# A spectral mixing layer and a gated feed-forward on one core: the order of loads, stores and weight sums in the opening

## The chip, the core and the metric

The kernel runs on one core of a Trainium2 chip. The metric is device time in microseconds, the median of several runs. A core has TensorE (PE in the profile, its weight loads PEld), VectorE (DVE), ScalarE (ACT), GpSimd (POOL) and SyncE (SP). Each engine takes its instructions in the order in which the kernel gives them; an instruction that waits holds all behind it on that engine. Transfers are issued by SyncE, ScalarE (their queues are SPq and ACTq) or GpSimd (POOLq), and the issue stands in the engine's order too.

## The reference

```python
def _attn_ref(x):                       # x: 8 x 3008 x 256
    X = np.fft.fft(x, axis=1)
    X = np.fft.fft(X, axis=2)
    return X.real.astype(np.float32)

def _moe_ref(x, w_in, w_out):           # 24064 x 256, 256 x 2048, 2048 x 256
    h = x @ w_in
    g = h * np.cos(h)
    return (g @ w_out).astype(np.float32)
```

The real part of a two-dimensional Fourier transform of each of 8 batches, over the 3008 positions and the 256 channels, goes through an input matrix, a gate h·cos(h) and an output matrix. All is float32.

## The kernel before, in words

**The transform over channels is folded into the weights.** `fold_weights(e, n)` (line 564) multiplies 512 columns of `w_in` by a cosine (`e` = 0) or sine (`e` = 1) matrix and leaves the result in `WC` or `WS`: four TensorE records of 512 columns and a ScalarE copy (lines 577, 583). For `e` = 1, row 0 belongs to the middle channel and is kept apart: VectorE copies it to `nrow[n]` (581), `send_wn(n)` (587) writes it to DRAM and `take_wn(n)` (591) reads it back across partitions into `wn`, four columns for each n. `load_w(n)` fetches the columns of `w_in`.

**The transform over positions is 47 times 64.** For batch 0, `load_x(b, p)` (189) loads half p of x, 16 of 32 columns from each of two sides, over SyncE (one column over GpSimd). `chunk(c)` (867) calls `fold(b, c, e)` (287): sums and differences of four columns on VectorE, and a ScalarE copy of one column (292). `first_half(b, c)` (414) multiplies the chunk by a 47-point matrix on TensorE and copies it to `zs` (450, 451); the chunk `DIRECT` (number 7) does without the fold. `middle(b, p)` (325) treats channel 128 of a whole half of x. `store_z(b, c, far)` (457) writes a chunk to DRAM: the near part (four of 24 output groups) first, over GpSimd for chunks 0 to 3 and over ScalarE and SyncE for the rest, the far part later over SyncE. `load_z` (482) reads it back with the axes exchanged, and `second_half(b, g)` (490) does the 64-point part for one of six groups of output rows: eight TensorE records (497), a ScalarE copy (508 or 514) and, for group 0 of batch 0, a small VectorE copy (512).

**The feed-forward runs in steps.** A step is one group of up to 256 rows by 256 of the 2048 inner columns: 8 batches x 6 groups x 8 = 384 steps. A step's accumulator H is seeded with 0.25 plus the product of middle channel and row weights: by ScalarE in `seed(s)` (629, 635) from `nb` and `wn`, or for the first two steps by VectorE and one-row matmuls in `fill_first` and `seed_first` (643, 647; 651). `mm1` (660, 665) adds the two matrix products; ScalarE and VectorE compute h·cos(h) (676 to 731); `mm2` (733, 755) multiplies by `w_out`. That matrix is used in sums of its quarters, which `combine_w2(f0, f1)` (617, 625) makes on VectorE for the inner columns f0 to f1 (eight in all) after `load_w2`. `combine_w2` is four instructions for each call.

**The order is written out by hand.** Lines 879 to 920 give the opening: `keep_busy` (603, matmuls on constants), the weight sums, the chunks, the stores, `combine_w2(0, 2)`, `load_z`, the later loads, `combine_w2(2, 4)` and `(4, 6)`, then `second_half(0, 0)`. The prologue (936 to 973) interleaves the first three steps by hand; `spread_norm` (524) broadcasts a row for them. The loop (988) runs three steps deep: step t starts `mm1` of step t while `mm2` of step t − 3 runs. Lists hold what else a step issues: `opening`, `todo`, `between`, `early` (weight sums in steps 3 and 4) and `aside`, GpSimd work that is made to start behind a given VectorE instruction of the step (`beside`, 979). `transform(b)` (535) puts batch b's loads, folds and halves into these lists; batch 1's first loads (`load_later_x`, 165) go out from step 2 on, over GpSimd for p = 0.

Of the kernel before, what the change touches and what calls it, by code (L numbers as in the profile page):

```python
# [29 lines left out]
XP = 4 * IP  # L30
# [104 lines left out]
def kernel(  # L135
# [29 lines left out]
    def load_later_x(b, p, s, set_):  # L165
# [4 lines left out]
        for k in range(7):  # L170
# [8 lines left out]
            queue = nc.gpsimd if b == 1 and p == 0 else nc.sync  # L179
# [9 lines left out]
    def load_x(b, p):  # L189
        xv = xs[p][0 : 16 * STEP].rearrange("(e g) c -> e g c", g=STEP)  # L190
        i0 = XP * p
        def load(queue, g, c0, c1, cols, **more):
            for m in range(3):
# [3 lines left out]
                    in_=x_r[b, 16 * m : 16 * m + k, cols],  # L197
# [12 lines left out]
    wr = [  # L210
# [3 lines left out]
    wr = [[w[:, 512 * i : 512 * i + 512] for i in range(2)] for w in wr]  # L214
# [5 lines left out]
    def load_w(q):  # L220
        for i in range(2):
            nc.sync.dma_start(
                out=wr[q][i],
                in_=moe_w_in[128 * i : 128 * i + 128, 512 * q : 512 * q + 512],
            )
# [22 lines left out]
    load_w(0)  # L248
# [8 lines left out]
    load_x(0, 0)  # L257
# [3 lines left out]
    load_x(0, 1)  # L261
# [3 lines left out]
    load_w(2)  # L265
# [21 lines left out]
    def fold(b, c, e):  # L287
# [3 lines left out]
        if e == 0:  # L291
            nc.scalar.copy(out=fv[:, 0, :, 0], in_=xv[:, :, 0])
# [164 lines left out]
    def store_z(b, c, far):  # L457
# [15 lines left out]
        for e in range(2):  # L473
            queue = nc.sync if far or (e == 0 and c in (4, 7)) else nc.scalar
# [60 lines left out]
    def transform(b):  # L535
# [28 lines left out]
    def fold_weights(e, n, tag="M"):  # L564
        W = WS if e else WC
        pw = psum("pw", tag)
        for i in range(2):
# [6 lines left out]
            )  # L574
        cols = slice(512 * n, 512 * n + 512)
        if e:
# [3 lines left out]
            nrow[n] = spool.tile([128, 512], FP, tag="pq", bufs=8, name="nrow")  # L580
            nc.vector.tensor_copy(out=nrow[n][0:1, :], in_=pw[0:1, :])
        else:
            nc.scalar.copy(out=W[:, cols], in_=pw)

    wds = {}

    def send_wn(n):
        wds[n] = dpool.tile([1, 512], FP, tag="wd", bufs=4, name="wd")
        nc.sync.dma_start(out=wds[n], in_=nrow[n][0:1, :])

    def take_wn(n):
        nc.sync.dma_start(
# [23 lines left out]

    def combine_w2(f0, f1):
        add, sub = ALU.add, ALU.subtract
        for dst, a, b, op in (
            (vx[:, 0], wv[:, 0, 1], wv[:, 0, 0], sub),  # L620
            (vx[:, 1], wv[:, 0, 1], wv[:, 1, 1], add),
            (vx[:, 2], vx[:, 0], wv[:, 1, 1], add),
# [454 lines left out]
```

## Time and profile before

| | |
|---|---|
| median of three runs | 1958.84 us (1954.87 to 1960.34) |
| the profiled execution, its own time | 1954.01 us |
| span of its profile | 1952.2 us |
| mean granted clock of TensorE | 0.994 |
| DMA, mean over the span | 46 GB/s |
| DMA between 5 and 10 us | 279 GB/s |

A profile line is read as: start and duration in us, the engine, the line of the kernel, the instruction, what it writes and reads, shape, how often; in brackets the idle time of the engine before it and what ended that. TensorE works one float32 matmul off in two records. Groups of one line (by shape) show their total and the mean in ns. The granted clock is a share of full speed.

### The profile page before, as it was taken

How to read it: one execution, taken by the hardware profiler on the slowest of the kernel's cores; microseconds unless marked ns; L12 is line 12 of the kernel's file. 1: busy time of each engine (PE TensorE's matmuls, PEld its weight loads, DVE VectorE, ACT ScalarE, POOL GpSimd, SP SyncE). 2: the span in 40 equal slices, each digit the busy share in tenths (PEclk: the TensorE clock that was granted, in tenths of full speed). 3: DMA queues.
4: the chain of work that ended last, by engine and by line, in shares of the span. 5: the costliest groups of instructions: out<-in, count | busy, mean ns of one | idle time of the engine just before them, and what ended most of it. 6: DMA issues, size and time to landing. Idle time of an engine off the chain costs nothing.

```text
span 1952.2 us, 30563 instructions
## 1 busy us (share of the span) xinstructions
PE 1927.7 (99%) x9534; PEld 1693.5 (87%) x9534; DVE 1780.4 (91%) x3348; ACT 1530.1 (78%) x2884; POOL 397.4 (20%) x465
## 2 busy tenths in 40 slices
PE   7999999999999999999999999999999999999998
PEld 3888889888998889988899888988889888898887
DVE  4889999999999998999989999899999999999998
ACT  3688878888788788887878888788887888788775
POOL 5022202222022211222112221122211222111101
PEclk8999999999999999999999999999999999999999
DMA  8221131012200121101211122110231000110000
GB/s 219 77 57 37 49 91 26 19 39 65 67 24 23 41 76 52 25 24 46 82 37 27 26 53 75 34 31 24 52 84 30 24 22 24 54 28 10 12 22 22
DMA packets 160753, 89.36 MB, mean 46 GB/s; under 512 B 109172, under 2 KB 155403, under 8 KB 158123
## 3 DMA queue, kind: packets, MB, share of 16 engines
q1 hardware_dynamic: 158655, 85.37, 16.8%
q0 software_dynamic: 1536, 1.81, 0.4%
q8 instruction: 76, 1.25, 0.3%
q14 instruction: 86, 0.70, 0.1%
q10 hardware_dynamic: 400, 0.23, 0.0%
HBM read 50.07 MB, written 37.28 MB: 45 GB/s over the span
## 4 chain that ended last, share of the span: by engine, by line
PE 96%; DVE 1%; DMA 1%; SPq 0%; issue 0%; ACT 0%; ACTq 0%; DVEq 0%
PE M L755 57%; PE H L665 34%; PE pb L497 2%; PE pz L387 2%; DMA w<-in_moe_w_out_dram 0%; PE pz L347 0%; DMA xp<-in_x_dram 0%; PE pz L445 0%; PE pw L568 0%; DVE r L710 0%; DVE S L721 0%; SPq L862 0%; PE H L651 0%; PE M L387 0%; SPq L195 0%
## 5 line engine op out<-in xcount | busy, mean ns | idle before, releaser
L755 PE MATMUL M<-S,VX 128*128 128x256 f32 (+1 forms) x2304 | 612.3, 375 | 0.0
L755 PEld LDWEIGHTS M<-S,VX 128*128 128x128 f32 x2304 | 437.8, 190 | 49.9
L696 ACT ACTIVATE r<-H 128x512 f32<-128x512 f32 (+1 forms) x384 | 226.1, 589 | 265.0 <-DVE h L681 265.0
L706 ACT ACTIVATE r<-r 128x1024 f32<-128x1024 f32 (+1 forms) x384 | 394.7, 1028 | 22.9 <-DVE r L700 18.9
L665 PE MATMUL H<-pq,WC 128*128 128x256 f32 (+1 forms) x1536 | 396.1, 381 | 1.8 <-ACT H L635 1.8
L665 PE MATMUL H<-pq,WS 128*128 128x256 f32 (+1 forms) x1536 | 389.4, 376 | 0.0
L755 PE MATMUL M<-r,w 128*128 128x256 f32 (+1 forms) x1536 | 387.7, 375 | 0.0
L635 ACT ACTIVATE H<-nb,wn 128x256 f32<-128x256 f32 (+1 forms) x764 | 362.0, 474 | 16.1 <-DVE r L710 1.3
L681 DVE TENSOR_TENSOR h<-ew,H 128x512 f32<-128x512 f32 (+1 forms) x384 | 258.9, 674 | 103.6 <-PE H L665 73.2
L665 PEld LDWEIGHTS H<-pq,WC 128*128 128x128 f32 x1536 | 284.7, 191 | 52.9 <-ACT r L696 15.8
L755 PEld LDWEIGHTS M<-r,w 128*128 128x128 f32 x1536 | 300.2, 196 | 28.3 <-issue 0.7
L665 PEld LDWEIGHTS H<-pq,WS 128*128 128x128 f32 x1536 | 292.6, 191 | 34.5 <-ACT ew L676 0.5
L700 DVE SCALAR_TENSOR_TENSOR r<-r,H 128x512 f32<-128x512 f32 (+1 forms) x384 | 258.6, 673 | 30.0 <-ACT r L696 13.6
L676 ACT ACTIVATE ew<-H 128x512 f32<-128x512 f32 (+1 forms) x384 | 225.8, 588 | 61.8 <-PE H L665 53.2
L807 POOL TENSOR_TENSOR cb<-cb,mr 128x256 f32<-128x256 f32 (+3 forms) x188 | 158.3, 852 | 518.1 <-DVE S L731 479.9
L721 DVE TENSOR_TENSOR S<-r 128x512 f32<-128x512 f32 (+1 forms) x384 | 259.0, 674 | 0.1
L710 DVE SCALAR_TENSOR_TENSOR r<-H,r 128x512 f32<-128x512 f32 (+1 forms) x384 | 255.9, 667 | 3.0 <-ACT r L706 2.5
L700 DVE SCALAR_TENSOR_TENSOR r<-r,h 128x512 f32<-128x512 f32 (+1 forms) x384 | 258.5, 673 | 0.0
L710 DVE SCALAR_TENSOR_TENSOR r<-h,r 128x512 f32<-128x512 f32 (+1 forms) x384 | 258.0, 672 | 0.0
L696 ACT ACTIVATE r<-h 128x512 f32<-128x512 f32 (+1 forms) x384 | 236.0, 615 | 0.0
L306 POOL TENSOR_TENSOR xs<-xp 113x512 f32<-113x512 f32 x112 | 143.2, 1278 | 446.4 <-DVE S L731 443.2
L755 PE MATMUL M<-S,w 128*128 128x256 f32 (+1 forms) x768 | 225.6, 375 | 1.1 <-DVE S L731 1.1
(103 smaller groups left out, 1581.5 us busy)
## 6 DMA issues: line engine op xcount, KB each, us to landing
out_dram<-ob SPq DMA_DIRECT2D x728, 32.0 KB
xp<-in_x_dram SPq DMA_DIRECT2D x250, 56.0 KB
z<-zd SPq DMA_DIRECT2D x8, 1280.0 KB
zd<-zs SPq DMA_DIRECT2D x224, 40.0 KB
nb<-nd SPq DMA_DIRECT2D x40, 128.0 KB
zd<-zs SPq DMA_DIRECT2D x224, 8.0 KB
xp<-in_x_dram SPq DMA_DIRECT2D x52, 48.0 KB
w<-in_moe_w_out_dram SPq DMA_DIRECT2D x4, 512.0 KB
```

Source lines behind the costliest of these rows:

```text
L306: return nc.gpsimd.tensor_tensor(out=xs2[e][0:XL], in0=xv[:, 0], in1=xv[:, 1], op=ALU.subtract if e else ALU.add,)
L635: nc.scalar.activation(out=s.H[:, u * T : u * T + T], in_=s.nb[:, 0:T], func=AF.Copy, bias=0.25, scale=wn[:, f : f + 1],)
L665: nc.tensor.matmul(s.H[:, u * T : u * T + T], lhsT=W[:, 128 * f : 128 * f + 128], rhs=s.pq[:, e * T : e * T + T], start=False, stop=True, ...
L676: nc.scalar.mul(out=s.ew[:, 0 : 2 * s.T], in_=s.H[:, 0 : 2 * s.T], mul=2.0)
L681: nc.vector.tensor_tensor(out=s.h[:, 0 : 2 * T].rearrange("p (u t) -> p u t", u=2)[:, :, ::-1], in0=s.ew[:, 0 : 2 * T].rearrange("p (u t) ...
L696: nc.scalar.activation(out=r, in_=h, func=AF.Copy, bias=BIG, scale=1.0)
L700: nc.vector.scalar_tensor_tensor(out=r, in0=r, scalar=-BIG, in1=h, op0=ALU.add, op1=ALU.subtract)
L706: nc.scalar.activation(out=r, in_=r, func=AF.Sin, bias=0.0, scale=SIN_SCALE)
L710: nc.vector.scalar_tensor_tensor(out=r, in0=h, scalar=-0.25, in1=r, op0=ALU.add, op1=ALU.mult)
L721: return nc.vector.tensor_tensor(out=sv[:, 0:2], in0=gv[:, 2:3].to_broadcast([128, 2, T]), in1=gv[:, 0:4:3], op=ALU.subtract,)
L755: nc.tensor.matmul(acc[key][m // 2][:, 256 * (m % 2) : 256 * (m % 2) + T], lhsT=w, rhs=a, start=first, stop=s.fp == 7, skip_group_check=True,)
L807: return nc.gpsimd.tensor_tensor(out=o, in0=a, in1=b, op=ALU.subtract if less else ALU.add)
```

## The change

- `load_x` takes a range of columns and a side. The second side goes over ScalarE's queue (for a range that starts at 0); the first half of x goes ahead of the first weight columns; the second half is loaded in two ranges. Contiguous runs are up to 4096 bytes instead of 1024 in one piece.
- `load_w(0..2)` is one transfer instead of two. `load_w(2)` moves from the first loads to a place behind `load_z` and `load_w2(2, 4)`.
- Eight filling matmuls instead of two; the two weight sums of n = 0 leave the start: the sine one stands before the fifth chunk, its row copy and the cosine one behind the last. The sine sum of n = 2 moves into the prologue, the cosine one to its end; the cosine sum of n = 3 from step 4 to step 5.
- Chunks run in the order 0 to 5, 7, 6 instead of 0 to 3, 7, 4 to 6. The copy of one column moves from ScalarE to VectorE.
- Near stores: ScalarE issues two instead of six, SyncE six.
- The row weights go to DRAM and back over GpSimd's queue, each pair together.
- `second_half(0, 0)` comes ahead of `combine_w2(2, 4)`. The sums for columns 4 to 8 run on GpSimd, one column in each of steps 3 to 6.
- Of batch 1's first loads seven stay on GpSimd; the others go to SyncE, at step 3 at the earliest. `load_w2(6, 8)` moves behind the far part of z.

```diff
-            queue = nc.gpsimd if b == 1 and p == 0 else nc.sync
+            queue = nc.gpsimd if b == 1 and p == s == set_ == 0 else nc.sync
...
-    def load_x(b, p):
+    def load_x(p, c0, c1, side):
...
+        queue = nc.scalar if side and not c0 else nc.sync
...
-        load(nc.sync, 0, 0, XP, slice(i0, i0 + XP), max_dma_last_dim=1024)
-        c0 = 0 if p else 1
-        load(nc.sync, 3, c0, XP, slice(64 - i0 - c0, 64 - i0 - XP, -1))
-        if p == 0:
+        if side == 0:
+            load(nc.sync, 0, c0, c1, slice(i0 + c0, i0 + c1), max_dma_last_dim=4096)
+            return
+        skip = 1 if p == c0 == 0 else 0
+        load(queue, 3, c0 + skip, c1, slice(64 - i0 - c0 - skip, 64 - i0 - c1, -1))
+        if skip:
             load(nc.gpsimd, 3, 0, 1, slice(32, 33))
...
     nc.sync.dma_start(out=LCS, in_=LCS_dr.ap())
-    load_w(0)
...
-    load_x(0, 0)
+    for side in range(2):
+        load_x(0, 0, XP, side)
...
-    load_x(0, 1)
+    load_w(0)
+    for c0 in (0, XP // 2):
+        for side in range(2):
+            load_x(1, c0, c0 + XP // 2, side)
     load_bj(0, 512)
     load_w(1)
     load_w2(0, 2)
-    load_w(2)
...
-            nc.scalar.copy(out=fv[:, 0, :, 0], in_=xv[:, :, 0])
+            nc.vector.tensor_copy(out=fv[:, 0, :, 0], in_=xv[:, :, 0])
...
-            queue = nc.sync if far or (e == 0 and c in (4, 7)) else nc.scalar
+            queue = nc.scalar if not far and e and c in (5, 6) else nc.sync
...
-                at(o + k, load_later_x, b, p, k % 2, k // 2)
+                at(max(o + k, LAG) if b == 1 and k else o + k, load_later_x, b, p, k % 2, k // 2)
...
-        nc.sync.dma_start(out=wds[n], in_=nrow[n][0:1, :])
+        nc.gpsimd.dma_start(out=wds[n], in_=nrow[n][0:1, :])
...
-        nc.sync.dma_start(
+        nc.gpsimd.dma_start(
             out=wn[:, 4 * n : 4 * n + 4], in_=wds[n].rearrange("o (q p) -> (o p) q", p=128)
...
-    keep_busy(2, "H", 512)
-    fold_weights(1, 0, "H")
-    fold_weights(0, 0, "H")
-    order = [c for c in range(NCH) if c < 4] + [DIRECT] + [c for c in range(4, NCH) if c != DIRECT]
+    keep_busy(8, "H", 512)
+    order = [0, 1, 2, 3, 4, 5, DIRECT, 6]
     folded = [c for c in order if c != DIRECT]
     chunk(folded.pop(0))
     for k, c in enumerate(order):
-        if c == DIRECT:
+        if k == 4:
             middle(0, 1)
-        elif folded:
+        if c != DIRECT and folded:
             chunk(folded.pop(0))
+        if k == 4:
+            late = fold_weights(1, 0, "H")
+            keep_fold(*late)
         first_half(0, c)
         store_z(0, c, 0)
     clear_later()
-    send_wn(0)
+    keep_row(*late)
+    fold(0, 0, "H")
     for s in steps[0:2]:
         fill_first(s)
+    send_wn(0)
+    take_wn(0)
     combine_w2(0, 2)
-    fold_weights(1, 1)
-    fold_weights(0, 1)
+    fold(1, 1)
     send_wn(1)
+    take_wn(1)
+    fold(0, 1)
     load_z(0, 0)
-    fold_weights(1, 2)
     load_w2(2, 4)
+    load_w(2)
     load_w2(4, 6)
-    take_wn(1)
-    send_wn(2)
-    take_wn(0)
     load_w(3)
-    load_w2(6, 8)
-    for c in range(NCH // 2):
-        store_z(0, c, 1)
-    take_wn(2)
-    for c in range(NCH // 2, NCH):
+    for c in range(NCH):
         store_z(0, c, 1)
     load_z(0, 1)
     load_bj(512, 1024)
+    load_w2(6, 8)
     load_bj(1024, NJ * 128)
     load_v()
+    second_half(0, 0)
     combine_w2(2, 4)
-    combine_w2(4, 6)
-    second_half(0, 0)
...
-        3: ((combine_w2, 6, 7), (send_wn, 3)),
-        4: ((combine_w2, 7, 8), (take_wn, 3)),
+        3: ((send_wn, 3), (take_wn, 3)),
...
+    for f in range(4, 8):
+        for dst, a, b, less in w2_sums:
+            aside.setdefault(f - 1, []).append((add, dst[:, f], a[:, f], b[:, f], less))
+    early = {3: (1, 3, "fft"), 5: (0, 3, "fft")}
...
     mm1(s0, 1)
     seed(s2)
+    late = fold_weights(1, 2)
     dve_h(s0)
     act_round(s0, 0)
     act_round(s0, 1)
     seed_first(s1)
     mm1(s1, 0)
-    act_e(s1)
+    keep_fold(*late)
     dve_frac(s0, 0)
     dve_frac(s0, 1)
+    keep_row(*late)
+    send_wn(2)
+    take_wn(2)
+    act_sin(s0)
+    act_e(s1)
     mm1(s2, 0)
-    act_sin(s0)
     mm1(s1, 1)
     act_e(s2)
-    fold_weights(0, 2)
...
     mm1(s2, 1)
+    keep_fold(*fold_weights(0, 2))
```

After the change the name `fold` stands for a weight sum with its copies; the fold of a chunk is called `fold_chunk`. `keep_fold` is the ScalarE copy of a weight sum, `keep_row` the VectorE copy of its row 0.

More of the change, by code (lines that the diff above doesn't have):

```diff
@@ L213 @@
     ]
-    wr = [[w[:, 512 * i : 512 * i + 512] for i in range(2)] for w in wr]
+    wr = [[w[:, 512 * i : 512 * i + 512] for i in range(2)] for w in staged]
     xs2 = [cpool.tile([128, 2 * ND], FP, tag=f"xs{e}", name="xs") for e in range(2)]
@@ L615 @@
     wv = w2.rearrange("p (f u c j) -> p u j f c", u=2, j=2, c=128)
-    def combine_w2(f0, f1):
[L618 to L622, printed above, removed]
-            (vx[:, 3], wv[:, 1, 0], vx[:, 2], sub),
-        ):
+    w2_sums = (
+        (vx[:, 0], wv[:, 0, 1], wv[:, 0, 0], True),
+        (vx[:, 1], wv[:, 0, 1], wv[:, 1, 1], False),
+        (vx[:, 2], vx[:, 0], wv[:, 1, 1], False),
+        (vx[:, 3], wv[:, 1, 0], vx[:, 2], True),
+    )
+    def combine_w2(f0, f1):
+        for dst, a, b, less in w2_sums:
             nc.vector.tensor_tensor(
-                out=dst[:, f0:f1], in0=a[:, f0:f1], in1=b[:, f0:f1], op=op
+                out=dst[:, f0:f1],
+                in0=a[:, f0:f1],
+                in1=b[:, f0:f1],
+                op=ALU.subtract if less else ALU.add,
             )
@@ L930 @@
     }
-    early = {3: (1, 3, "fft"), 4: (0, 3, "fft")}
+    for f in range(4, 8):
+        for dst, a, b, less in w2_sums:
+            aside.setdefault(f - 1, []).append((add, dst[:, f], a[:, f], b[:, f], less))
+    early = {3: (1, 3, "fft"), 5: (0, 3, "fft")}
     n = len(steps)
```

38 lines of the change are left out of this document (25 added, 13 removed).

## The prediction

> **What bounds the kernel now.** I read the page first: its shares, then its chain of work that ended last.
>
> ```profile
> PE 1927.7 (99%) x9534; PEld 1693.5 (87%) x9534; DVE 1780.4 (91%) x3348; ACT 1530.1 (78%) x2884; POOL 397.4 (20%) x465
> PE 96%; DVE 1%; DMA 1%; SPq 0%; issue 0%; ACT 0%; ACTq 0%; DVEq 0%
> ```
>
> TensorE is busy for 99% of the span and carries 96% of the chain. Nothing in the steady part can be won by an edit to the opening; what the opening can give is an earlier moment at which TensorE runs without gaps. So I read TensorE's timeline of the first 82 us (start, duration, what, and idle time in brackets).
>
> ```profile
> 3.60 3.78 PE L606 MATMUL pd<-VX 128*128 128x512 f32 x4 [3.60 <-DVE VX L251]
> 7.18 4.56 PE L568 MATMUL pw<-wr,LCS 128*128 128x512 f32 x8
> 13.90 0.40 PE L442 MATMUL pz<-xf,LCS 128*64 128x128 f32 x2 [0.86 <-DVE xf L293]
> 19.13 0.20 PE L329 MATMUL pm<-xp,LCS 110*64 110x16 f32 x1
> 20.90 1.10 PE L445 MATMUL pz<-xf,LCS 128*64 128x512 f32 x4
> 24.12 1.08 PE L445 MATMUL pz<-xf,LCS 128*64 128x512 f32 x4 [0.18 <-ACT xf L292]
> 25.13 5.42 PE L568 MATMUL pw<-wr,LCS 128*128 128x512 f32 x12
> 32.79 1.91 PE L497 MATMUL pb<-BJ,z 128*128 128x128 f32 x8 [2.25 <-DMA z<-zd]
> 40.23 1.86 PE L651 MATMUL H<-pq,nrow 1*128 1x225 f32 x4 [5.52 <-DVE pq L512]
> 46.66 1.86 PE L651 MATMUL H<-pq,nrow 1*128 1x225 f32 x4
> 55.02 0.92 PE L665 MATMUL H<-pq,WS 128*128 128x225 f32 x4
> 57.13 1.03 PE L665 MATMUL H<-pq,WC 128*128 128x225 f32 x4 [1.19 <-ACT H L635]
> 75.30 1.05 PE L497 MATMUL pb<-BJ,z 128*128 128x128 f32 x8
> 80.38 0.92 PE L665 MATMUL H<-pq,WC 128*128 128x225 f32 x4
> ```
>
> The largest hole is ahead of 40.23: 5.52 us, put down to the copy at line 512. VectorE's and ScalarE's timelines say why that copy was late.
>
> ```profile
> 34.74 0.48 ACT L508 COPY pq<-pb 128x384 f32<-128x384 f32 x1 [3.47 <-PE pb L497]
> 35.38 0.76 DVE L625 TENSOR_TENSOR VX<-w 128x256 f32<-128x256 f32 x2 [3.40 <-DMA w<-in_moe_w_out_dram]
> 38.48 0.76 DVE L625 TENSOR_TENSOR VX<-w 128x256 f32<-128x256 f32 x2 [1.55 <-DMA w<-in_moe_w_out_dram]
> 39.96 0.22 DVE L512 COPY pq<-pb 128x66 f32<-128x66 f32 x1
> ```
>
> The copy takes 0.22 us and its data are there at 34.70 (32.79 + 1.91). It stands on VectorE's queue behind two groups of output-weight sums (L625), and each of these waits for its weights. The second thing to read is the clock, in windows of 3.41 us whose edges lie on its two changes (busy us, records, clock, DMA share, GB/s).
>
> ```profile
> 5.69:9.10 3.41, 3.41 (x5) 1.00 1.02 282
> 12.51:15.93 3.42, 2.28 (x13) 1.00 1.14 243
> 29.58:32.99 3.41, 1.16 (x4) 1.00 0.85 212
> 32.99:36.41 3.42, 1.72 (x8) 0.50 1.18 261
> 46.65:50.06 3.41, 3.41 (x9) 0.50 0.63 157
> 50.06:53.47 3.41, 3.41 (x10) 0.50 0.45 131
> 53.47:56.89 3.42, 2.47 (x8) 1.00 0.82 281
> ```
>
> The granted clock falls to 0.50 after a window with 1.16 us of work, and comes back 20.48 us (six windows) later, after one filled with full matmuls. A window half filled with the one-row matmuls of line 651 (46.65 to 50.06) did not bring it back, and one with 2.28 us of work (12.51 to 15.93) did not lose it. So the prologue from 40.23 to 57.13, 16.90 us, runs for 13 us at half speed.
>
> **The change, part by part.**
>
> *x on two queues, the first weights behind it.* The transfers ahead of the first sums lose the 0.5 MB of the first weight columns, 1.9 us at the 282 GB/s of the first of these windows. But TensorE now first runs eight filling matmuls, 16 records: twelve such records ended at 11.74 (7.18 + 4.56), and four more at 0.45 (5.42/12) end at 13.5. The first half cannot begin before, and began at 13.90. Value: 0; bounds −1.5 us (clock up sooner, the line shorter) to +0.5.
>
> *The order of chunks; the column copy on VectorE; first weight sums moved between chunks.* VectorE's pair of folds paces chunks; its row with SyncE's and GpSimd's issues stands here:
>
> ```profile
> 13.07 4.87 DVE L293 TENSOR_TENSOR xf<-xp 110x508 f32<-110x508 f32 x8 [1.61 <-DMA xp<-in_x_dram]
> 22.58 10.81 POOL L180 DMA_DIRECT2D xp<-in_x_dram x20 [0.99 <-PE pz L445]
> 29.27 0.35 SPq L486 DMA_DIRECT2D z<-zd  x1
> ```
>
> A chunk costs VectorE 1.22 (4.87/4) plus at most 0.22 for the copy (the row of line 512 is larger), and TensorE 1.08. Two chunks being folded by 13.9, four are through at about 18.3, against 19.1. The middle column of the second half still needs all of x, as at 19.13: two parts do not shorten that. Then follow 0.2 (middle), 1.8 (four records of weight sums, newly in the line), three chunks at 1.08 and the unfolded one at about 1.8 (19.13 to 20.90): 7.0 us, so 25.3 from 18.3 or 26.1 from 19.1. I take 25.6; before it was 25.20. Loss 0.4, bounds 0.1 to 0.9.
>
> *Nothing large beside z; the stores over three queues.* From the end of the first half to the landing of z were 7.6 us (25.20 to 32.79), 3.52 of them from the issue at 29.27. GpSimd's twenty x loads, issued from 22.58 on, ran beside it; now seven of these loads come much later and the rest go to SyncE. Six of the eight late stores were issued by ScalarE; now two are. I take 0.8 off (0.3 issue, 0.5 transfer), bounds 0 and 1.5: z at 32.4.
>
> *The second half's copy ahead of the sums.* From z to the end of the ScalarE copy were 2.43 us (34.74 + 0.48 − 32.79); VectorE's small copy ends within that. TensorE's prologue thus starts at 34.9 instead of 40.23: **5.3 us won.** What is late next is ScalarE's copy. The sums of columns 2 to 4 stay on VectorE, 1.6 us, in the 5 us in which it waited for TensorE's broadcast; if their weights came after 40, they would hold the line.
>
> *The third weight sums move into the prologue.* Their sine half left the stage before z (the count of records there stays twelve, 31.0 is its end) and comes after the first 6.43 us of the prologue (40.23 to 46.66). At half clock its four records cost 3.8 (the row of 3.60), 3.4 if the clock rises within them; full matmuls fill the line from about 4.7 us on, so I let it rise at their end. Behind it: seeds 0.95, sixteen records of 0.23 (0.92/4) 3.7, the cosine half 1.8. Sum 6.43 + 3.4 + 0.95 + 3.7 + 1.8 = 16.3, against 16.90: **0.6 won**, between 5.4 (clock never low: seeds 1.9, 24 records 5.5, the broadcast 0.55, two halves of weight sums 3.6, so 11.5) and −2.9 (rising late: the seeds at 1.86, and twelve records at 0.45 instead of 0.23).
>
> *Late output-weight sums on GpSimd.* VectorE loses the group at 38.48 and these two:
>
> ```profile
> 65.99 0.49 DVE L625 TENSOR_TENSOR VX<-w 128x128 f32<-128x128 f32 x2
> 70.75 0.50 DVE L625 TENSOR_TENSOR VX<-w 128x128 f32<-128x128 f32 x2
> L807 POOL TENSOR_TENSOR cb<-mr 128x225 f32<-128x225 f32 x2 | 1.3, 664 | 4.7 <-DVE S L731 4.7
> ```
>
> With the chained sums behind them each took about 1.07. But TensorE was idle for only 1.2 us between 57.13 and 80.38, and its work there stays; **0.4 won** (0 to 1.2). On GpSimd a sum costs less than 664 ns, sixteen of them 10.6 us at most, in four steps, before the matmuls three steps later want them.
>
> *Weight rows over GpSimd's queue.* Eight small transfers in pairs, each pair a trip to memory and back on which GpSimd waits. Landing times of GpSimd's DMAs, from three views (a loaded window, a quiet one, all x loads):
>
> ```profile
> zd<-zs POOLq DMA_DIRECT2D x6, 16.0 KB, 5.0
> xp<-in_x_dram POOLq DMA_DIRECT2D x5, 56.0 KB, 2.8
> DMA to landing us min/median/max: 2.2/4.2/8.9
> ```
>
> When the rows are there and when ScalarE wants them comes from these:
>
> ```profile
> 27.87 0.68 DVE L581 COPY nrow<-pw 1x512 f32<-1x512 f32 x1 [2.18 <-ACT WS L577]
> 45.40 0.94 ACT L635 ACTIVATE H<-nb,wn 128x225 f32<-128x225 f32 x2 [0.92 <-DVE nb L529]
> 63.00 0.94 ACT L635 ACTIVATE H<-nb,wn 128x225 f32<-128x225 f32 x2 [1.28 <-DVE r L710]
> ```
>
> The second pair starts when its row is copied, about 30.5 (31.0 less one group of weight sums, plus two copies of 0.7), under load; at 4.2 each it lands at 38.9. ScalarE wants it 5.2 us into the prologue (45.40 − 40.23), at 40.1. It fits by 1.2. The third starts at 46.1 (34.9, 9.8 to the end of the sine half, two copies) and is wanted 5.9 into step 3 (63.00 − 57.13), at 51.2 + 5.9 = 57.1. The fourth stands behind four sums and is wanted at step 5, where TensorE has some 7 us of work in hand. I take 0; bounds 0 and 15.0 (below). Behind these waits on GpSimd stand the next batch's loads and the late sums, wanted from step 7 on.
>
> ```profile
> L180 POOL DMA_DIRECT2D xp<-in_x_dram x28: 504/565/647, 22.6 to 42.1; - x28
> ```
>
> VectorE's sums of line 625 ran beside these issues (shortest, median, longest ns) and lengthened none beyond 647 ns. The Trainium skill, SBUF — State Buffer, section "SBUF: two separate sides", says that a DMA issued by GpSimd cannot get its descriptors written while VectorE holds the shared port: 620 ns alone became about 3100 ns. By that, an estimate of 2.5 us more for each row transfer. The row above does not show it, but line 625 is not the copy that the page measured.
>
> **Sum.** 5.3 + 0.6 + 0.4 = 6.3 us. The profiled execution took 1954.01 us (span 1952.2), so 1947.7. The median of the runs is 4.8 above it, at 1958.84: the same sum gives 1952.5 there. I cannot see whether the 4.8 us lie in the opening, where the filling matmuls would remove them (the short gap ahead of 13.90 is a place where another run could lose its clock), or elsewhere. I take the middle, **1950.0**.
>
> **Rivals.**
>
> *The clock never falls.* The gap ahead of z shrinks from 2.25 to about 1.4, so a window may keep over 1.16 us of work. Then the second half's matmuls take 1.05 and the prologue 11.5, and the second row pair is wanted at about 37, so it is 1.9 late. Gain 6.3 + 0.8 + 4.8 − 1.9 = 10.0: 1944.0 from the profiled run, 1948.8 from the median. Against it: the one-row seeds count little, as 46.65 to 50.06 shows. The Trainium skill, TensorE: Matmul & The Clock Gate, on what is actually happening, gives a free-running window of about 3.4 us. The trace agrees: 20.48 us is six of them; by that rule the phase may differ from run to run.
>
> *It rises late.* The seeds of the second step cut the block of full matmuls (5.2 us, a window and a half) before a whole window fits. The prologue takes 3.5 us longer: gain 2.8, 1951.2 to 1956.0.
>
> *Slower: the rows hold ScalarE.* Let a row transfer land after L. The second pair stalls ScalarE 2L − 9.6, the third 2L − 11.0; above L = 6.7 us the 6.3 us are gone, and at 8.9 the stalls are 15.0: 8.7 slower, 1967.5. For it: 8.9 was seen on this queue. Against it: those were loads of 56 KB queued behind one another; these are 2 KB. By the lock of the Trainium skill's page SBUF — State Buffer (section as above) an L of 4.2 would become an estimated 6.7, and the gain nothing.
>
> **How the numbers follow.** Forecast 0.43, clock never falling 0.24, rising late 0.23, rows late 0.10. The range takes the first three, 1943.5 to 1957.0. Faster by over 0.3% (5.9 us, about what a measurement of this kernel can tell from no change) is below 1953.0: most of the forecast, all of the second and a fifth of the third case: 0.67. Slower is most of the fourth, 0.07. Within is what is left, 0.26.
>
> **What would show it.** Right: line 508's copy followed by line 651's matmuls within 0.5 us, at 34 to 36; no L625 rows between; step 3 at 50 to 52; step 7 near 74. The clock windows from 31 on decide between the first three cases. A wait of line 635 on the rows' DMA decides for the fourth. I am wrong if z lands after 34, if line 508 waits for something new, or if steps 3 to 6 grow.

## The result, and the profile after

The changed kernel takes 1950.65 us in the median of six runs (1949.91 to 1953.97), the kernel before 1958.69 us in the six runs beside it (1954.87 to 1960.34). The ratio is 0.9964, with a 95% interval of 0.9951 to 0.9977: faster by 8.0 us. The two profiled executions lie closer together: 1949.91 us (span 1948.1) against 1954.01 (1952.2), 4.1 us. That the medians gained twice as much as the profiles is one of the things to be explained. All ratios leave out the one slow run that there was, of 4119.77 us in experiment 9, in which every matmul took about twice its time.

First the page of the changed kernel, its shares and its chain of work:

```profile
PE 1929.5 (99%) x9546; PEld 1693.7 (87%) x9546; DVE 1778.5 (91%) x3343; ACT 1528.7 (78%) x2877; POOL 397.8 (20%) x468
PE 96%; issue 1%; DMA 1%; DVE 1%; POOL 0%; SPq 0%; ACT 0%; ACTq 0%; DVEq 0%; POOLq 0%
```

TensorE still carries 96% of the chain; what changed lies in the first 80 us. TensorE's timeline of the changed kernel (start, duration, what, idle time in brackets; lines have moved: 442 is now 452, 497 is 507, 651 is 676, 665 is 690):

```profile
13.92 0.40 PE L452 MATMUL pz<-xf,LCS 128*64 128x128 f32 x2 [0.73 <-DVE xf L303]
...
21.27 0.26 PE L339 MATMUL pm<-xp,LCS 110*64 110x16 f32 x2 [1.97 <-issue]
...
26.85 1.08 PE L455 MATMUL pz<-xf,LCS 128*64 128x512 f32 x4
...
33.22 1.13 PE L507 MATMUL pb<-BJ,z 128*128 128x128 f32 x8
35.18 1.02 PE L676 MATMUL H<-pq,nrow 1*128 1x225 f32 x4 [0.83 <-DVE pq L522]
...
37.09 0.64 PE L538 MATMUL pn<-pq,ones 1*128 1x225 f32 x2
...
53.27 0.92 PE L690 MATMUL H<-pq,WC 128*128 128x225 f32 x4
...
76.01 0.92 PE L690 MATMUL H<-pq,WC 128*128 128x225 f32 x4
```

Compare with the prediction's rows of before, mark by mark. The first chunk starts at 13.92 (13.90). The middle column, which needs all of x, comes at 21.27 (19.13), and the first half ends at 27.93 (25.20): later by 2.7. TensorE takes up z at 33.22 with no gap ahead of it (32.79 with one). The prologue starts at 35.18 (40.23): 5.05 won. Step 3 starts at 53.27 (57.13): 3.86 are left, so the prologue lost 1.2. Step 7 starts at 76.01 (80.38): 4.37, which is about the 4.1 by which the spans differ.

ScalarE's timeline shows the copy that now ends the wait, and a new wait of 6.23 us in the prologue:

```profile
34.38 0.48 ACT L518 COPY pq<-pb 128x384 f32<-128x384 f32 x1 [0.48 <-PE pb L507]
37.20 0.55 ACT L701 ACTIVATE ew<-H 128x450 f32<-128x450 f32 x1 [2.33 <-PE H L690]
43.98 0.94 ACT L660 ACTIVATE H<-nb,wn 128x225 f32<-128x225 f32 x2 [6.23 <-DMA wn<-wd]
```

Line 660 is the old 635, the seed of the third step: it waits for the second row pair. GpSimd's timeline has that pair's trip (line 610 writes the row to DRAM, 613 reads it back), with the first pair beside it:

```profile
26.72 0.52 POOL L610 DMA_DIRECT2D wd<-nrow  x1 [4.99 <-DVE nrow L598]
28.58 0.80 POOL L613 DMA_DIRECT2D wn<-wd  x1 [1.34 <-DMA wd<-nrow]
33.29 0.52 POOL L610 DMA_DIRECT2D wd<-nrow  x1 [3.92 <-DVE nrow L598]
40.52 0.79 POOL L613 DMA_DIRECT2D wn<-wd  x1 [6.71 <-DMA wd<-nrow]
```

The first pair's way out took 1.86 us (26.72 to 28.58), the second's 7.23 (33.29 to 40.52), and its way back 3.46 (40.52 to 43.98): 10.7 us for 2 KB there and back. The granted clock, in windows whose edges lie on its changes (busy us and records of PE, PEld, DVE, ACT, POOL; clock; DMA share; GB/s):

```profile
31.42:34.83 3.41, 2.93 (x13) 1.52 (x11) 0.68 (x1) 1.72 (x3) 0.52 (x1) 1.00 0.85 278
34.83:38.24 3.41, 3.00 (x12) 2.08 (x13) 2.05 (x6) 0.58 (x2) 0.00 (x0) 1.00 0.96 293
38.24:41.65 3.41, 3.41 (x8) 1.72 (x6) 0.62 (x1) 0.00 (x0) 0.79 (x1) 0.50 0.81 263
41.65:45.07 3.42, 2.60 (x11) 1.45 (x9) 0.00 (x0) 1.06 (x3) 0.00 (x0) 1.00 0.65 170
```

The window that lost its clock before, the one ahead of z, now holds 2.93 us of work and keeps it. The prologue starts at full clock, loses it at 38.24, gets it back and loses it again from 45.07 to 51.89. Busy time alone does not tell when: the window from 34.83, after which the clock fell, held 3.00 us of work, more than the one before it, which kept it. But 1.66 us of the 3.00 were one-row matmuls (1.02 of line 676 and 0.64 of line 538), and the 2.93 us before held none. This fits the prediction's "the one-row seeds count little"; no run here tries it alone. The fast start of the prologue only brought ScalarE sooner to a row that had not landed.

**The account of the profiled executions:** 5.05 at the start, −1.2 in the prologue, 0.5 in steps 3 to 6 (22.74 us instead of 23.25): 4.4 at step 7.

### The profile page after: what moved, and what is told of

Same layout as the page of the kernel before. It is cut to its first block, busy times and chain, and to the rows that moved or that the text cites. A ratio compares the mean times of both kernels' runs of the same rounds, so it can differ in the third digit from the quotient of the medians.

```text
span 1948.1 us, 30580 instructions
## 1 busy us (share of the span) xinstructions
PE 1929.5 (99%) x9546; PEld 1693.7 (87%) x9546; DVE 1778.5 (91%) x3343; ACT 1528.7 (78%) x2877; POOL 397.8 (20%) x468
## 4 chain that ended last, share of the span: by engine, by line
PE 96%; issue 1%; DMA 1%; DVE 1%; POOL 0%; SPq 0%; ACT 0%; ACTq 0%; DVEq 0%; POOLq 0%
PE M L780 58%; PE H L690 34%; PE pb L507 2%; PE pz L397 2%; DMA wn<-wd 0%; DMA xp<-in_x_dram 0%; PE pz L357 0%; DMA wd<-nrow 0%; SPq L887 0%; PE M L397 0%; POOL zd L487 0%; PE pz L385 0%; DVE r L735 0%; PE pz L455 0%; DVE S L746 0%
```

## The experiments

The theory at this point: the gain comes from the second half's copy standing ahead of the sums (T1); it is cut by x's second half, which lands 2.1 later in two parts per side (T2), and by the second row pair, which ScalarE waits for (T3). The rivals: the filling matmuls or the later loads of batch 1 make the gain; the rows cost nothing in the end. All times are medians; each ratio is that of a kernel's runs to runs of the kernel before beside them on the same chip, whose median was 1956.95 (22 runs, experiments 1 to 4), 1957.47 (22 runs, 5 to 8) and 1957.66 (nine runs, 9 to 12). An interval of a ratio is some 2 to 2.5 us wide on either side, so where variants of the changed kernel differ by less, only their traces speak. The changed kernel itself was not run again beside its variants: a difference from its 1950.65 us is one between runs at different times, between which the median of the kernel before moved by up to 1.7 us. Each trace is of one execution.

**1. x's second half in one part.**

```diff
-    for c0 in (0, XP // 2):
-        for side in range(2):
-            load_x(1, c0, c0 + XP // 2, side)
+    for side in range(2):
+        load_x(1, 0, XP, side)
```

> The changed kernel, with the second half of x in one range for each side (six transfers instead of twelve). Theory A, x's second half came 2 us later (21.3 us instead of 19.1) because the issue of a hardware transfer waits until the eighth one before it has landed, so that nine small ones took 10.8 us to issue: now it is there at about 19.2, the first half ends near 25.8 instead of 27.9, the prologue starts near 33.2 instead of 35.2, and the time is about 2 us lower than the changed kernel's. Theory B, the rate of the DMA engines sets it: x at 21.3 as before, time within 0.5 us.

1949.94 us (1948.7 to 1952.68), ratio 0.9962 [0.9949, 0.9974]. SyncE's issues of x and TensorE's middle column, first of the changed kernel, then of this one:

```profile
7.30 10.82 SPq L197 DMA_DIRECT2D xp<-in_x_dram  x9
```

```profile
7.06 6.18 SPq L197 DMA_DIRECT2D xp<-in_x_dram  x3
```

```profile
19.66 0.26 PE L338 MATMUL pm<-xp,LCS 110*64 110x16 f32 x2 [0.81 <-ACT zs L459]
33.49 1.02 PE L675 MATMUL H<-pq,nrow 1*128 1x225 f32 x4 [0.83 <-DVE pq L521]
```

Nine issues kept SyncE until 18.12, three until 13.24, and all of x is there 1.6 us sooner (19.66). The prologue starts 1.7 sooner and step 3 still 1.2 sooner. T2 holds for the opening; why nine issues are slower than three stands in the last section. In time it is 0.7, which no interval here can tell from nothing.

**2. The third step seeded like the first two**, by one-row matmuls from rows that VectorE has, so that ScalarE needs the second pair only for step 3.

```diff
-    for s in steps[0:2]:
+    for s in steps[0:3]:
         fill_first(s)
...
-    seed(s2)
...
     act_e(s1)
+    seed_first(s2)
     mm1(s2, 0)
```

> The changed kernel, with the third step seeded like the first two (VectorE fills it with 0.25, one-row matmuls add the product), so that ScalarE needs no row weights before step 3. Theory A, the trip of the second row pair over GpSimd's queue holds the prologue (ScalarE waited 6.2 us for it): the wait goes, step 3 starts at 48 to 49 us instead of 53.3, and the time falls by 4 to 5 us. Theory B, the prologue is held by the clock and by the chain of VectorE and ScalarE anyway: step 3 at 52 or later, time within 1 us of the changed kernel's.

1951.24 us (1947.34 to 1952.87), ratio 0.9966 [0.9954, 0.9978]. TensorE, then ScalarE:

```profile
36.55 1.02 PE L676 MATMUL H<-pq,nrow 1*128 1x225 f32 x4 [0.83 <-DVE pq L522]
...
50.66 0.92 PE L690 MATMUL H<-pq,WC 128*128 128x225 f32 x4
...
74.45 0.92 PE L690 MATMUL H<-pq,WC 128*128 128x225 f32 x4
```

```profile
68.76 0.94 ACT L660 ACTIVATE H<-nb,wn 128x225 f32<-128x225 f32 x2 [3.13 <-DMA wn<-wd]
```

The prologue takes 14.1 us (36.55 to 50.66) instead of 18.1: the wait for the second pair cost 4.0, as T3 says. But the time is the same. In this execution the prologue started 1.4 later (TensorE lost its clock from 22.07 to 25.48, after a gap of 1.85 ahead of the middle column). ScalarE still waits for the third and the fourth pair (1.45 at 55.67, and 3.13; in the changed kernel 2.74 at 59.56, and 1.79), and step 7 begins only 1.6 sooner. The rows are a chain of their own; to free one link moves the wait to the next.

**3. The sums on VectorE ahead of the second half again.**

```diff
-    second_half(0, 0)
     combine_w2(2, 4)
+    combine_w2(4, 6)
+    second_half(0, 0)
...
-    for f in range(4, 8):
+    for f in range(6, 8):
```

(The sums of columns 4 and 5 thus go from GpSimd back to VectorE too.)

> The changed kernel, with the output-weight sums of columns 2 to 6 on VectorE ahead of the second half again, as before the change. Theory A, the order frees the prologue's start, but the row pair gives most of it back: the prologue starts 3 to 5 us later (38 to 40 us), while ScalarE's wait for the row weights shrinks by as much; the time is 1 to 2 us above the changed kernel's. Theory B, the start counts in full: 4 to 5 us above the changed kernel's.

1952.88 us (1952.2 to 1954.22), ratio 0.998 [0.9971, 0.9989]. VectorE and TensorE:

```profile
38.06 0.76 DVE L647 TENSOR_TENSOR VX<-w 128x256 f32<-128x256 f32 x2 [2.28 <-DMA w<-in_moe_w_out_dram]
...
39.53 0.22 DVE L522 COPY pq<-pb 128x66 f32<-128x66 f32 x1
```

```profile
39.81 1.86 PE L676 MATMUL H<-pq,nrow 1*128 1x225 f32 x4 [6.01 <-DVE pq L522]
```

The hole of before is back (6.01 us, for the same copy behind the same sums), and the prologue starts at 39.81. T1 holds: the place of the copy is worth 4.6 us at the start. That it is the place and not the engine of the sums shows in experiment 10, where VectorE makes these sums behind the copy and the prologue starts at 34.62. Of the 4.6 some 2.2 show in the medians (3.1 by the ratios), because a prologue that starts later no longer waits for the second pair (it takes 14.9 us).

**4. The kernel before with four filling matmuls instead of two.**

```diff
-    keep_busy(2, "H", 512)
+    keep_busy(4, "H", 512)
```

> The kernel before, with four filling matmuls instead of two, so that TensorE is busy until 13.5 us like in the changed kernel. Theory A, some runs of the kernel before lose TensorE's clock in the gap ahead of 13.9 us, and this is why their median lies 4.7 us above the profiled run: the median falls by 3 to 5 us, to about 1954.5, and the spread of the runs shrinks. Theory B, the spread comes from elsewhere: median within 1.5 us of the kernel before.

1956.88 us (1955.13 to 1959.65), ratio 0.9999 [0.999, 1.0008]. Filling does nothing for the time. This profiled execution (1958.88 us) was one of the longer ones. VectorE and TensorE again,

```profile
44.34 0.76 DVE L625 TENSOR_TENSOR VX<-w 128x256 f32<-128x256 f32 x2 [5.70 <-DMA w<-in_moe_w_out_dram]
```

```profile
34.93 2.08 PE L497 MATMUL pb<-BJ,z 128*128 128x128 f32 x8 [4.33 <-DMA z<-zd]
...
46.08 1.86 PE L651 MATMUL H<-pq,nrow 1*128 1x225 f32 x4 [9.07 <-DVE pq L512]
```

z landed 2.1 later than in the profile of before, the last output weights 5.9 later (44.34 against 38.48), and the prologue started at 46.08 instead of 40.23. So one long and one short execution differ in when z and the weights land, and the profile that the prediction read was of a short one. That the runs of the kernel before vary by this is an inference from these two; experiment 7 tests it.

**5. The second row pair on ScalarE's queue.**

```diff
-        nc.gpsimd.dma_start(out=wds[n], in_=nrow[n][0:1, :])
+        (nc.scalar if n == 1 else nc.gpsimd).dma_start(out=wds[n], in_=nrow[n][0:1, :])
...
     send_wn(1)
-    take_wn(1)
     fold(0, 1)
     load_z(0, 0)
+    second_half(0, 0)
+    take_wn(1)
...
-    second_half(0, 0)
```

(`take_wn(1)` goes over ScalarE too.)

> The changed kernel, with the second row pair on ScalarE's queue: the row goes out at the same time (about 33.3 us), and its way back is issued behind the second half's copy. Theory A, a transfer of GpSimd's queue is slow itself when the engines are loaded (7.2 us for the row, 3.5 for its way back): on ScalarE's queue both take 1 to 2 us, the row weights are there before ScalarE wants them, the wait of 6.2 us goes, the prologue takes 14 us instead of 18.1 and step 3 starts near 49.5. Theory B, any queue is as slow beside the large loads: ScalarE stands until about 44 us, and the prologue takes 18 us as before. The time: A 1 to 3 us under the changed kernel's, because the later pairs still hold steps 3 and 5; B the same.

1951.16 us (1949.63 to 1952.36), ratio 0.9969 [0.9957, 0.998]. ScalarE's timeline:

```profile
32.69 0.24 ACTq L610 DMA_DIRECT2D wd<-nrow  x1
...
37.37 0.41 ACTq L613 DMA_DIRECT2D wn<-wd  x1
...
42.77 0.94 ACT L660 ACTIVATE H<-nb,wn 128x225 f32<-128x225 f32 x2 [4.39 <-DMA wn<-wd]
```

The trip took 10.1 us (32.69 to 42.77), against 10.7 over GpSimd: the way out was 2.5 shorter (4.68), the way back 1.9 longer (5.40). The queue that issues the rows is not what makes the trip slow.

**6. x over SyncE's queue alone** (with x's second half in one part).

```diff
-        queue = nc.scalar if side and not c0 else nc.sync
+        queue = nc.sync
```

> The changed kernel with the second half of x in one range (as in x_one_part), and all of x on SyncE's queue. Theory A, two queues are worth little, because filling matmuls hold TensorE until 12.7 to 13.5 us and the engines move both queues at one rate: first chunk within 0.7 us of 13.5, x's second half within 1 us of 19.7, time within 0.7 us of x_one_part. Theory B, the second queue halves the time of issue: without it the first chunk and the second half of x come 1.5 to 3 us later, and the time is 1 to 2 us higher.

1954.48 us (1951.95 to 1956.14), ratio 0.9987 [0.9978, 0.9996]: 4.5 us above experiment 1. TensorE:

```profile
22.00 0.37 PE L338 MATMUL pm<-xp,LCS 110*64 110x16 f32 x2 [3.25 <-DMA xp<-in_x_dram]
...
37.37 1.02 PE L675 MATMUL H<-pq,nrow 1*128 1x225 f32 x4 [0.83 <-DVE pq L521]
```

The first chunk is not later (13.38), but all of x is there 2.3 us later than with two queues (22.00 against 19.66), TensorE loses its clock in the wait (from 21.74 on), and the prologue starts 3.9 later. The prediction had given the second queue no value of its own. The Trainium skill, DMA: Bandwidth & Descriptors, section "Issuing engines are not separate DMA queues", says that issuing on several engines only saves the time of the issue, usually small beside the transfer. Here it was 2.3 us of landing, with the DMA engines busy in both kernels (share 1.05 and 1.03 of 16 engines between 14 and 17 us). It was not the time of the issue: SyncE was through with x at 12.97 here and at 13.24 in experiment 1. Between 17 and 20 us the engines moved 234 GB/s here and 289 there. What in the order of the transfers makes it so much stays open.

**7. The kernel before with the next batch's loads as in the changed one.**

```diff
-            queue = nc.gpsimd if b == 1 and p == 0 else nc.sync
+            queue = nc.gpsimd if b == 1 and p == s == set_ == 0 else nc.sync
...
-                at(o + k, load_later_x, b, p, k % 2, k // 2)
+                at(max(o + k, LAG) if b == 1 and k else o + k, load_later_x, b, p, k % 2, k // 2)
```

> The kernel before, with the next batch's first loads as in the changed kernel: seven on GpSimd at step 2, the others on SyncE from step 3. Theory A, these loads delay the landing of z and of the output weights, by an amount that differs from run to run (the prologue started at 40.2 us in one profile and at 46.1 in another), and this is why the median gains more than the profiled runs do: the prologue starts at 37 to 40, the median falls by 2 to 4 us to 1953 to 1955, and the spread shrinks. Theory B, the loads do not matter: median within 1 us of the kernel before.

1953.76 us (1951.99 to 1955.08), ratio 0.998 [0.9971, 0.9989]: 3.7 us off the median. TensorE, SyncE and ScalarE:

```profile
37.56 1.86 PE L651 MATMUL H<-pq,nrow 1*128 1x225 f32 x4 [4.41 <-DVE pq L512]
```

```profile
59.86 10.27 SPq L180 DMA_DIRECT2D xp<-in_x_dram  x21
```

```profile
74.54 0.94 ACT L635 ACTIVATE H<-nb,wn 128x225 f32<-128x225 f32 x2 [5.14 <-DMA wn<-wd]
```

z lands sooner (31.98), the output weights too, the prologue starts at 37.56, and all this although the last row pair now stands behind 21 loads on SyncE (issued at 70.17) and holds ScalarE for 5.14. Its profiled execution (1953.52) is only 0.5 below that of before. So this part of the change is worth 3.7 us to the median and almost nothing beside the early-landing execution that was profiled. The 3.2 between the two are most of the 3.9 by which the medians gained more (8.0) than the profiles (4.1), as far as one profile of each kernel can tell.

**8. Three edits together:** experiments 1 and 2, and the fourth row pair sent right after its sums.

```diff
-        3: ((send_wn, 3), (take_wn, 3)),
...
                 fold(*early[t])
+                if t == 3:
+                    send_wn(3)
+                    take_wn(3)
```

> The changed kernel with the second half of x in one range, the third step seeded by matmuls, and the fourth row pair ahead of GpSimd's sums in step 3. Theory A, the row pairs took back what the earlier start gave, each in turn: with the second not needed and the fourth earlier, step 3 starts at 47 to 48 us, no wait of line 635's successor is over 1.5 us, step 7 starts at 71 to 72 and the time is 1945 to 1947. Theory B, steps 3 to 7 are held by VectorE and TensorE: step 7 stays at 74 or later and the time at 1949 to 1950.

1948.99 us (1946.62 to 1950.02), ratio 0.9958 [0.9945, 0.997]. TensorE and ScalarE:

```profile
71.36 0.92 PE L689 MATMUL H<-pq,WC 128*128 128x225 f32 x4
...
78.69 1.13 PE L689 MATMUL H<-pq,WC 128*128 128x256 f32 x4 [2.41 <-ACT H L659]
```

```profile
77.65 0.99 ACT L659 ACTIVATE H<-nb,wn 128x256 f32<-128x256 f32 x2 [4.78 <-DMA nb<-nd]
```

Step 7 starts 4.65 us sooner than in the changed kernel (71.36 against 76.01), step 8 only 1.5 (78.69 against 80.20), and the span is 0.9 shorter. At step 8 ScalarE waits for another small transfer, the second half's norm, whose two issues stand on SyncE behind the loads of batch 1 until 72.75 and 74.62. Most of the gain was turned into a new wait.

**9. Four edits: fourteen instead of seven of those loads on GpSimd.**

```diff
-            queue = nc.gpsimd if b == 1 and p == s == set_ == 0 else nc.sync
+            queue = nc.gpsimd if b == 1 and p == s == 0 else nc.sync
```

> The version with three edits (x's second half in one part, third step seeded from the first rows, fourth row pair sent right after its sums), and fourteen instead of seven of the next batch's x loads on GpSimd's queue. Theory A: in the version with three edits the 2.41 us that TensorE waited at step 8 came from the two small transfers of the second half's norm, which stood on SyncE behind 21 loads and four more; with 14 of them there they are issued at about 66 instead of 72.7, the wait goes, and 1.5 to 2.4 us come off: 1946.6 to 1947.5. Rival B: the gain is taken by another wait (the sums of the last output-weight columns, now behind seven more issues and the fourth row pair on GpSimd, or those issues beside TensorE's first steps): 1949, as with three edits.

1945.9 us in the median of five runs (four of 1945.19 to 1947.83, and the one of 4119.77), ratio 0.9942 [0.9929, 0.9956]. The four lie below every run of both kernels, though the changed kernel was not run beside them. The time is a little under the 1946.6 to 1947.5 of theory A. The one profile is of the run of 4119.77 us and none of it is used, so that the wait at step 8 is what went was not seen.

**10. The late sums back on VectorE**, behind the second half's copies.

```diff
     second_half(0, 0)
     combine_w2(2, 4)
+    combine_w2(4, 6)
...
-        3: ((send_wn, 3), (take_wn, 3)),
+        3: ((combine_w2, 6, 7), (send_wn, 3), (take_wn, 3)),
+        4: ((combine_w2, 7, 8),),
...
-    for f in range(4, 8):
-        for dst, a, b, less in w2_sums:
-            aside.setdefault(f - 1, []).append((add, dst[:, f], a[:, f], b[:, f], less))
```

> The changed kernel with the late output-weight sums back on VectorE (columns 4 to 6 behind the others ahead of the prologue, but after the second half's copies; 6 and 7 at steps 3 and 4), and no sums on GpSimd. Theory A (the prediction): moving them is worth 0.4 us, so 1951.1, with VectorE later by about 1 us in steps 3 and 4. Rival B: the move cost as much as it saved, because GpSimd's sums hold back the fourth row pair (issued at 62.50 behind four sums) and stretch VectorE's operations at step 5; without it the wait of 1.79 us at step 6 goes, and the time is 1949 to 1950.5. Rival C: the weights of columns 4 to 6 land late and hold VectorE ahead of the first step's work: step 3 later by 1 to 3 us, 1952 to 1954.

1950.18 us (1948.97 to 1952.03), ratio 0.9964 [0.9952, 0.9977], the same as the changed kernel. From TensorE's rows of it, steps 3 and 7:

```profile
51.96 0.92 PE L690 MATMUL H<-pq,WC 128*128 128x225 f32 x4
...
75.31 0.92 PE L690 MATMUL H<-pq,WC 128*128 128x225 f32 x4
```

Steps 3 to 6 take 23.35 us here and 22.74 in the changed kernel: 0.6 for GpSimd, near the 0.4 predicted, though its waits for the rows at steps 4 and 6 stand against it there. ScalarE's wait at step 6, which here is gone, was this one of the changed kernel:

```profile
70.08 0.94 ACT L660 ACTIVATE H<-nb,wn 128x225 f32<-128x225 f32 x2 [1.79 <-DMA wn<-wd]
```

Neither shows in the time. Whether the move gains or loses was not settled; it is under 2.5 us.

**11. Fewer large loads beside the second row pair.**

```diff
     load_w(2)
-    load_w2(4, 6)
-    load_w(3)
     for c in range(NCH):
         store_z(0, c, 1)
+    load_w(3)
+    load_w2(4, 6)
```

> The changed kernel with 1 MB of weights (output-weight columns 4 to 6 and the fourth input-weight columns) issued behind the sixteen stores instead of ahead of them, so that only 1 MB of large loads is in flight when the second row pair starts at 33.3. Theory A (the small transfers are slow because the large loads fill the DMA engines): the trip of 10.7 us shortens by about the 3.3 us that 1 MB takes at some 300 GB/s, ScalarE's wait of 6.23 us falls to about 3, and step 3 starts at 50 to 50.5 instead of 53.27. Time 1949 to 1950.7, since earlier runs gave most of such a gain back behind step 3. Rival B (it is the queue of GpSimd, or the sixteen stores beside it): the pair lands at 43.5 to 44.5 as before, and the time is 1950.7 or worse, with the fourth input-weight columns late at step 3.

1950.37 us (1950.01 to 1951.34), ratio 0.9964 [0.995, 0.9978]. GpSimd and ScalarE:

```profile
32.68 0.52 POOL L610 DMA_DIRECT2D wd<-nrow  x1 [3.92 <-DVE nrow L598]
```

```profile
42.91 0.94 ACT L660 ACTIVATE H<-nb,wn 128x225 f32<-128x225 f32 x2 [5.54 <-DMA wn<-wd]
```

The trip took 10.2 us (32.68 to 42.91) with 1 MB less ahead of it, against 10.7. I had expected 3.3 off; my theory that the bytes of the large loads make it slow fell. The DMA engines were less full, too: between 36 and 40 us their share was 0.69 at 202 GB/s, against 0.97 at 319 in the changed kernel. What is left beside the rows are the sixteen stores of small pieces, which started 2.1 us sooner here (31.34); that they are the cause was not tried. Step 3 began at 51.91 (theory A: 50 to 50.5), and the time did not move.

**12. Pieces of 1024 instead of 4096 bytes** (with x's second half in one part).

```diff
-            load(nc.sync, 0, c0, c1, slice(i0 + c0, i0 + c1), max_dma_last_dim=4096)
+            load(nc.sync, 0, c0, c1, slice(i0 + c0, i0 + c1), max_dma_last_dim=1024)
```

> The changed kernel with x's second half in one part per side, and pieces of at most 1024 bytes in the loads of the first side as in the kernel before, instead of 4096. Theory A (piece size does not matter here): first chunk at 13.9, middle column at 19.1 to 19.7, time 1949.9 as with 4096. Rival B (longer pieces bring x sooner): the middle column comes at 20.5 or later, and the time rises by about as much, to 1951.

1950.31 us (1948.66 to 1952.8), ratio 0.9965 [0.9952, 0.9977]; the middle column at 20.42, first chunk 13.50. It lies between the two theories (0.8 later than in experiment 1, 0.4 us in time), and both are about what executions differ by: with the loads of the changed kernel the column came at 21.27, 20.91 and 20.53 in three of them (changed kernel, experiments 2 and 3).

## Why the prediction was right, and where it was not

The predicted 1950.0 is 0.65 from the measured 1950.65, but by steps of which several missed in opposite directions.

- **Second half's copy ahead of the sums, 5.3 won at the start:** right in its mechanism. 5.05 measured, start at 35.18 (forecast 34.9), row by row as described: line 518's copy, 522's, line 676 within 0.32 us of the copy's end, no sums between. Experiment 3 shows the cause. That the start came so near is in part luck: TensorE took up z 0.8 later than forecast, and from there to the end of the copy were 1.64 us (33.22 to 34.86) instead of 2.43, since the clock had stayed up.
- **x on two queues, value 0; the middle column "as at 19.13":** half right. The first chunk did not move (13.92). But the middle column came 2.1 later, since two parts per side made nine issues on SyncE out of three (experiment 1 gives 1.6 of it back). And the second queue, which I did not weigh at all, was worth 2.3 us of landing (experiment 6). The end of the first half was 27.93 instead of the 25.6 that I took.
- **Nothing large beside z, 0.8 off:** too small. From the end of the first half to z were 5.3 us (27.93 to 33.22) instead of 7.6: 2.3 off, which paid for most of the loss above. Of these 1.5 lay ahead of z's issue (30.51, 2.6 behind the end of the first half, instead of 4.1) and 0.8 behind it; I had taken 0.3 and 0.5. I put z at 32.4; it was taken up at 33.22.
- **The prologue, 0.6 won:** wrong; it lost 1.2 (18.09 us against 16.3 forecast). The step that failed is that of the weight rows, "It fits by 1.2", with 0 taken and the bounds 0 and 15.0. The second row started at 33.29 instead of 30.5, because the first half ended later, and its two transfers took 10.7 instead of 2 x 4.2 = 8.4; and with the clock up at first, ScalarE wanted it at 37.75 and not at 40.1. It waited 6.23 us, and experiment 2 shows that this cost the prologue 4.0. The third pair took longer still, 12.1 us (47.45 to 59.56), and ScalarE waited 2.74 for it. So the rival in which the rows hold ScalarE happened at part of its size, together with the beginning of the rival in which the clock never falls: the one took what the other brought.
- **Its own signs:** the copy and line 676 at 34 to 36 came as said, with no sums between. Step 3 came at 53.27 and not at 50 to 52, step 7 at 76.01 and not near 74, and the wait of the seeds on the rows' DMA, the sign of the fourth case, was there.
- **The clock:** none of the three cases came as a whole. It stayed up at the start (the case "never falls"), fell at 38.24, was up for one window from 41.65, in which TensorE waited 0.82 us for the seeds, and was low again from 45.07 to 51.89.
- **Late sums on GpSimd, 0.4:** 0.5 in the trace for steps 3 to 6, and 0.6 in experiment 10 by trace; nothing that the times show.
- **The fourth pair "has some 7 us of work in hand":** wrong in small. Its way out was issued at 62.50, behind four sums, and ScalarE waited 1.79 us for it at step 6 (the row in experiment 10).
- **Profile or median:** I left open where the 4.8 us between them lie and took the middle. They lie in the opening, but not where I looked: more filling does nothing (experiment 4), the loads of batch 1 beside z and the output weights do (experiment 7, for most of it). Forecast from the profile: 1947.7, 2.2 below the profile after; from the median: 1952.5, 1.85 above the median after. Two misses stood against each other: the sum was 1.9 too large (6.3 against 4.4 at step 7), and the part that varies from run to run brought 3.2 that the sum did not hold (experiment 7: 3.7 in the median, 0.5 in the profile). That the middle met the result is owed to this, not to a right sum.

## What to carry over

Read not only which wait ends last, but what small transfer the next engine will want when that wait is gone, and start its chain from a trace row of the same kind beside the same traffic: 2 KB took 1.9 us in a quiet moment and 7.2 beside stores and loads. When one wait is removed and the time stays, look for the next link (the rows for the third step and for steps 4 and 6, then the norm at step 8): only the version with edits to all of them, four in number, reached 1945.9 us. And compare a profile with its median before using either: what differs from run to run is itself a thing that a change may remove.

## What was not expected of the hardware

- **Small transfers beside large ones.** The same write of one 2 KB row took 1.86 us at 26.72 and 7.23 at 33.29 over GpSimd's queue, and 4.68 over ScalarE's (experiment 5). 1 MB less of weights in flight changed the whole trip by 0.5 us only (experiment 11). What makes it slow stays open.
- **More, smaller issues slow the loading itself.** Three issues of x on SyncE kept it 6.18 us and nine 10.82. The stretch from 17 to 20 us, first of the changed kernel, then of experiment 1 (the last two columns are the DMA share and GB/s):

```profile
17.00:20.00 3.00, 2.30 (x8) 0.54 (x6) 3.00 (x8) 2.07 (x6) 2.76 (x6) 1.00 0.73 176
```

```profile
17.00:20.00 3.00, 2.19 (x9) 0.72 (x8) 1.08 (x4) 1.79 (x6) 2.62 (x6) 1.00 1.03 289
```

With nine issues the DMA engines are not full (0.73). SyncE's waits for earlier pieces of x are not the difference: they come to 5.2 us in the changed kernel and to 4.7 in experiment 1. The issues themselves are. The last seven stand almost back to back:

```profile
12.82 5.30 SPq L197 DMA_DIRECT2D xp<-in_x_dram  x7
```

These are 0.76 us each for 120 or 128 KB, an estimate of 168 GB/s, about the rate of the window. The trace shows what the waits are for: in this program the transfers of SyncE and ScalarE report their landing on eight semaphores in turn, and an issue stands until the transfer that had the same semaphore before it has landed. The issue at 12.82 began 0.02 us after the landing of the piece that ScalarE had issued at 4.52.
- **GpSimd's sums stretch VectorE's.** The changed kernel at step 5, VectorE's gate instruction alone at 63.02 and beside GpSimd's sums at 67.18, then one of these sums beside VectorE (67.96) and one alone (71.13):

```profile
63.02 0.62 DVE L725 SCALAR_TENSOR_TENSOR r<-r,h 128x450 f32<-128x450 f32 x1
...
67.18 1.36 DVE L725 SCALAR_TENSOR_TENSOR r<-r,h 128x450 f32<-128x450 f32 x1
```

```profile
67.96 0.90 POOL L832 TENSOR_TENSOR VX<-VX,w 128x128 f32<-128x128 f32 x1
...
71.13 0.46 POOL L832 TENSOR_TENSOR VX<-VX,w 128x128 f32<-128x128 f32 x1
```

Each of the two took about twice its time where they ran together: GpSimd's sums had been put behind another VectorE instruction of the step, but the wait for the fourth row pair delayed them into this one. The Trainium skill, SBUF — State Buffer, section "Who interferes with whom", says that a VectorE instruction with two inputs in SBUF contends with a GpSimd instruction that reads SBUF; these rows agree, with 1.36 against 0.62 us.
